# The seven-product stage of a fused attention and MoE kernel: g kept in PSUM, products in offset pairs

## Chip, cores and metric

One core of a Trainium2 chip. The metric is the device time of one execution in microseconds. Before the change the median of three runs is 555.94 us (554.25 to 556.14).

## The reference, cut to what matters

Windowed attention with sink tokens gives x, a soft mixture of experts turns x into its output, and a last layer follows. Only that last layer is changed. With n = 3072 tokens, model width 512 and inner width 2048:

```
c = row softmax of (x @ phi)              # 3072 x 32
x = c @ slot_out                          # 3072 x 512
h = x @ w_in                              # 3072 x 2048
g = h - tanh(h)
out = g @ w_out                           # 3072 x 512, float32
```

The kernel never forms x: it multiplies w_in with slot_out first and gets h from the 32 columns of c.

## The kernel before, in words

**Layout.** Output and g are held transposed: channels on the 128 partitions, tokens on the free axis. Inner channels come in 16 blocks f of 128. One h matmul (`cT`, `wst`, 96 rows: high and low parts of c and w stacked) gives one block of 128 inner channels by 512 tokens in one PSUM bank (`h_b`, two banks). ACT computes tanh in place and then u, a scaled square of it; DVE multiplies u and h to g (`g_mul`, L1280). g is split for TensorE into a rounded part gh (ACT, L1494 and L1601) and the rest gl = g - gh (L1451, which calls `arith`, L1444). gh and gl have five buffers each (`NG`). The weights w_out are loaded as 64-bit words, converted on DVE (L113 to L132, with a square on ACT), and split the same way into `whi` and `wlo`. One multiplication by g is three matmuls of 128 x 512: whi gh, wlo gh, whi gl.

**Regular steps.** The first 1024 tokens go in 32 steps (`steps`, L1194; N = 32): a step is one f, one chunk c of 512 tokens, four output blocks, 12 matmuls into `acc[0..3]`. A group of steps ends with an eviction of the four banks, added to a sum in SBUF (L1474 to L1491). Steps up to 5 are written out by hand (L1302); from step 6 on PE's work is ordered by the planner.

**Seven products.** The other 2048 tokens, in two halves (c = 1, 2) of 1024, use a scheme of seven products instead of eight (Winograd's form of Strassen's). A11, A12, A21, A22 are quarters of g (tokens halved, inner channels halved), S1 = A21 + A22, S2 = S1 - A11, S3 = A11 - A21, S4 = A12 - S2. On the weights' side T1 to T4 stand for B11 to B22 in the same way; T3 and T4 are prepared from w_out during the regular steps, T1 and T2 are split afresh at each use (`tsplit`, L1631). A product has 8 inner blocks i; a unit is one product and one i: 6 matmuls into two banks. There are 112 units. Before, they run as P4 and P5 alternating, then P7 and P1, then P6, P2 and P3 in turn, for each half; six banks accumulate (`acc`, `y_t`, `cv_t`), two hold h. At the end of each product its two banks are copied (ACT, L1668) or combined with earlier results (`comb`, L1623) and results are stored.

**Where g lies.** For the products g is written into one of 19 SBUF buffers (`place`, L1566). The low parts (L1450) and the sums S1 to S4 (L1595) then read two SBUF operands, and may go to POOL or DVE.

**What sets the order.** `_Order` (L142) is a list planner: each task has a due time, one or several engines with a cost from `US` (L59), and the buffers it reads and writes. `emit` simulates the engines and fixes each engine's program. The engines then run their programs in order, with semaphores. The due time of regular step i is 3.0 i, of product units 1.5 us apart (`op`, L1437). How far ahead of its use each stage stands is set by constants: `RL` and `WL` (L60, L61), and `TLAG` for the preparation of T3 and T4 (L1724). At an any-engine task the planner counts 0.69 us for DVE and 1.29 for POOL:

```
def arith(at, dst, a, b, rd, wr, alu=ALU.subtract, half=False, engs=("POOL", "DVE")):
    us = {"POOL": 0.67 if half else US["p"], "DVE": 0.4 if half else US["v"]}
    td.any_of(at, {e: (us[e], lambda e=e: names[e].tensor_tensor(dst, a, b, op=alu)) for e in engs}, rd, wr)
...
g = (g_b[k % 3], f"g{k % 3}")
...
add(t, "DVE", US["v"], [hn, un], [g[1]] + ([] if fast else ["z", "mk"]), lambda h=h, u=u, g=g: g_mul(h, u, g[0], fast))
```

A second copy of the program, for inputs that leave the small range of h or other window sizes, stands behind a branch that is not taken here (`fast` false).

Of the kernel before, what the change touches and what calls it, by code (L numbers as in the profile page):

```python
# [210 lines left out]
def tile_kernel(ctx: ExitStack, tc: tile.TileContext, qk, vv, v0, v0t, nw, phi, w1, w2,  # L211
# [17 lines left out]
    def run(ctx, fast):  # L229
# [1041 lines left out]
        def g_mul(h, u, g, small, fills=()):  # L1271
# [7 lines left out]
            if small:  # L1279
                DVE.tensor_tensor(g, u, h, op=ALU.mult)  # L1280
                fill()
            else:
                DVE.tensor_scalar(mk, u, TB * TB, None, op0=ALU.is_gt)
                DVE.tensor_scalar(z, u, TB * TB, None, op0=ALU.min)
                DVE.tensor_scalar(u, z, cg[6], None, op0=ALU.mult)
                for q in (5, 4, 3, 2, 1, 0):
                    DVE.scalar_tensor_tensor(u, u, cg[q], z, op0=ALU.add, op1=ALU.mult)
                fill()
                DVE.tensor_tensor(g, u, h, op=ALU.mult)
                ACT.activation(z, h, AF.Tanh)  # L1290
                DVE.tensor_tensor(z, h, z, op=ALU.subtract)
                DVE.copy_predicated(g, mk, z)
# [163 lines left out]
        for s in range(max(s0 - DL - 1, 0), N):  # L1456
            c, f, first, last = steps[s]
            t, x = op(s), s % NG
            gh, gl = gh_b[x], gl_b[x]
            wh, wl = whl[f]  # L1460
            W_ = [f"w{f}h", f"w{f}l"]
            for q in range(4):
                r = slice(P * q, P * q + P)

                def hi(q=q, r=r, wh=wh, wl=wl, gh=gh, first=first):
                    mm(acc[q], wh[:, r], gh, first, False)
                    mm(acc[q], wl[:, r], gh, False, False)
# [4 lines left out]
                add(t + 0.01 * q, "PE", 2 * US["mm"], [f"gh{x}"] + W_, [f"a{q}"], hi)
                add(t + (0.01 * q + 0.005 if last else 1.5 + 0.01 * q), "PE", US["mm"], [f"gl{x}"] + W_, [f"a{q}"], lo)
            if last:  # L1474
                fresh = (c, f) in ((0, 1), (1, 3))
                for q in range(4):
                    sp, o, b = sp_b[c % 2][q], acc[q], f"sp{c % 2}{q}"
                    at = t + 2.2 + 0.2 * q
                    if not fresh and (q % 2 == 0 or not fast):
                        add(at, "DVE", US["v"], [f"a{q}", b], [b], lambda sp=sp, o=o: DVE.tensor_tensor(sp, o, sp, op=ALU.add))  # L1480
                    elif q % 2 == fresh:
                        add(at, "DVE", US["v"], [f"a{q}"], [b], lambda sp=sp, o=o: DVE.tensor_copy(sp, o))
                    elif fresh:
                        add(at, "ACT", US["ev"], [f"a{q}"], [b], lambda sp=sp, o=o: ACT.copy(sp, o))
                    else:
                        m, n = (z, "z") if q == 1 else (mk.bitcast(F32), "mk")
                        add(at, "ACT", US["ev"], [f"a{q}"], [n], lambda m=m, o=o: ACT.copy(m, o))
                        add(at + 0.5, "POOL", US["p"], [n, b], [b], lambda sp=sp, m=m: POOL.tensor_tensor(sp, sp, m, op=ALU.add))
                    if f == 15:
                        add(at + 1.0, "SP", 0.1, [b], [f"out{c}{q}"],  # L1490
                            lambda sp=sp, q=q, c=c: SP.dma_start(out[P * q:P * q + P, CK * c:CK * c + CK], sp))  # L1491
            if s >= max(s0 - 1, 0):
                g = g_b[s % 3]
                add(t - RL["cast"], "ACT", US["cast"], [f"g{s % 3}"], [f"gh{x}"], lambda g=g, gh=gh: ACT.copy(gh, g))  # L1494
                split_lo(t - RL["lo"], g, f"g{s % 3}", x)

        prod = []
        for s in range(s0, N):
            prod.append((op(s), RL, s))
        need = {"A22": "P4", "A21": "P5", "A11": "P7", "A12": "P2"}  # L1500
        units = []
        for c in (1, 2):
            for a, n in ((0, 2), (2, 2), (4, 3)):
                units += [(c, MULT[a + j], i) for i in range(8) for j in range(n)]
        at_u = {(c, p[0], i): op(N + k) for k, (c, p, i) in enumerate(units)}
        gs = []
        for c in (1, 2):
            gs += [(c, a, i) for i in range(8) for a in ("A22", "A21")]
            gs += [(c, a, i) for a in ("A11", "A12") for i in range(8)]
        due = [at_u[c, need[a], i] - (1.5 if a in ("A21", "A11") else 0) for c, a, i in gs]  # L1510
        for j in range(len(gs) - 2, -1, -1):
            due[j] = min(due[j], due[j + 1] - GGAP)
        prod += [(t, WL, k) for t, k in zip(due, gs)]
        prod.sort(key=lambda e: e[0] - e[1]["h"])
        n = s0 + 1
        done = {}
        for t, L, k in prod:
            if L is RL and k == s0:
                done[k] = k
            elif not fast and L is RL and k == 1:  # L1520
                done[k] = k
            else:
                n = max(n, 1 if fast else 2)
                done[k] = n
                n += 1
        left = list(raw_f)
        blocks = {}

        def g_mul_at(k):
            if k in range(N):  # L1530
                return g_b[k % 3], f"g{k % 3}"
            return blocks[k]

        ev, muls = [], {}
        for t, L, k in prod:
            m = done[k]
            th = max(t - L["h"], muls.get(m - 2, -99.0) + 0.01)
            ta = max(t - L["act"], th + 0.3)
            tm = muls[m] = max(t - L["mul"], ta + 1.2, muls.get(m - 1, -99.0) + 0.01)
            assert tm < t - 4.7, (k, t, tm)  # L1540
            h, u, hn, un = h_b[m % 2], u_b[m % 3], f"h{m % 2}", f"u{m % 3}"
            if k in range(N):
                c, f = steps[k][:2]
                tok = CK * c
            else:
                c, a, i = k
                f = i + 8 * (a in ("A12", "A22"))
                tok = 1024 * c + CK * (a in ("A21", "A22"))
            x = f if f < 2 else 2 if f < 4 else 2 + f // 4
            if k not in range(s0 + (1 if fast else 2)):  # L1550
                add(th, "PE", US["h"], [f"wst{x}{q}" for q in range(3)], [hn],
                    lambda h=h, f=f, tok=tok: PE.matmul(h, w_of(f), cT[0:G3, tok:tok + CK], start=True, stop=True))  # L1552
            add(ta, "ACT", US["act"], [hn], [hn, un], lambda h=h, u=u: h_act(h, u, fast))
            ev.append((tm, "mul", k, (h, u, hn, un)))
        for k, (c, p, i) in enumerate(units):
            t = at_u[c, p[0], i]
            if p[1][0] == "S":
                ev.append((t - WL["sum"], "sum", (c, p[1], i), None))
            ev.append((t - WL["cast"], "cast", (c, p, i), N + k))
            ev.append((t - WL["lo"], "lo", (c, p, i), N + k))  # L1560
        ev.sort(key=lambda e: e[0])
        pool_, here = [(b, f"raw{b_}") for b_, b in enumerate(raw_f)], {}
        pool_ += [(b, n) for b, n in ((wf_b[8], "wfr0"), (wf_b[9], "wfr1"), (wf_b[10], "wfr2"), (cv_b[0], "cv0"))]
        pool_ += [(g_b[x], f"g{x}") for x in range(3)]

        def place(k):  # L1566
            here[k] = pool_.pop(0)

        for t, kind, k, arg in ev:
            if kind == "mul":  # L1570
                h, u, hn, un = arg
                if k in range(N):
                    g = (g_b[k % 3], f"g{k % 3}")
                else:
                    place(k)
                    g = here[k]
# [59 lines left out]
        for k, (c, p, i) in enumerate(units):  # L1636
# [11 lines left out]
            for ct in range(2):  # L1648
# [12 lines left out]
                if i < 7:  # L1661
                    continue
# [175 lines left out]
```

## Time and profile before

| | |
|---|---|
| median of three runs | 555.94 us |
| profiled execution, its own time | 555.75 us |
| span of its instructions | 554.0 us |
| busy, share of the span: PE, DVE, ACT, POOL | 90%, 84%, 71%, 65% |
| mean granted TensorE clock | 0.979 |

The span is the time from the first to the last instruction of the profiled execution. PE is TensorE's matmuls, PEld its weight loads, DVE VectorE, ACT ScalarE, POOL GpSimd, SPq the queue that issues the DMAs. Matmuls overlap in the pipeline: a matmul row lasts 0.39 us, but they start 0.23 us apart, so PE's busy share overstates its work and starts have to be counted. The clock is the granted share of full speed (1.00 is 2.4 GHz, 0.50 is 1.2 GHz).

### The profile page before, as it was taken

How to read it: one execution, taken by the hardware profiler on the slowest of the kernel's cores; microseconds unless marked ns; L12 is line 12 of the kernel's file. 1: busy time of each engine (PE TensorE's matmuls, PEld its weight loads, DVE VectorE, ACT ScalarE, POOL GpSimd, SP SyncE). 2: the span in 40 equal slices, each digit the busy share in tenths (PEclk: the TensorE clock that was granted, in tenths of full speed). 3: DMA queues.
4: the chain of work that ended last, by engine and by line, in shares of the span. 5: the costliest groups of instructions: out<-in, count | busy, mean ns of one | idle time of the engine just before them, and what ended most of it. 6: DMA issues, size and time to landing. Idle time of an engine off the chain costs nothing.

```text
span 554.0 us, 10289 instructions
## 1 busy us (share of the span) xinstructions
PE 496.3 (90%) x3554; PEld 337.3 (61%) x3554; DVE 466.6 (84%) x822; ACT 392.2 (71%) x1092; POOL 361.5 (65%) x383
## 2 busy tenths in 40 slices
PE   8798999999989998899898799998899989999991
PEld 4555556555545532466586567776578768776870
DVE  3999998998796496689997598889987998998676
ACT  4798998898895342388786569877688667857640
POOL 0466766656633000059999998698958798998972
PEclk9999999999999999899999889999999999999996
DMA  8979896434558999924310001200000021000004
GB/s 307 411 276 354 290 325 200 134 108 146 200 174 272 353 389 409 410 75 146 114 38 1 0 1 40 91 25 0 0 1 2 1 95 58 0 1 1 1 1 155
DMA packets 21995, 77.60 MB, mean 140 GB/s; under 512 B 2866, under 2 KB 4018, under 8 KB 20018
## 3 DMA queue, kind: packets, MB, share of 16 engines
q1 hardware_dynamic: 21938, 76.89, 38.2%
q8 instruction: 29, 0.48, 0.4%
q14 instruction: 28, 0.23, 0.1%
HBM read 70.59 MB, written 6.29 MB: 139 GB/s over the span
## 4 chain that ended last, share of the span: by engine, by line
PE 33%; DVE 25%; POOL 18%; DMA 9%; ACT 8%; issue 6%; SPq 0%; DVEq 0%; POOLq 0%; ACTq 0%
PE o L1454 12%; DMA w<-in_w 4%; DVE gl L1444 4%; POOL gl L1444 3%; PE av L728 3%; ACT w L664 3%; PE y L1454 3%; POOL wx L1444 3%; PE cvt L1454 3%; DVE mx L655 3%; PE h L1552 3%; PE o L1037 2%; DMA w<-in_qk 2%; DVE w L710 2%; DVE w L1444 2%
## 5 line engine op out<-in xcount | busy, mean ns | idle before, releaser
L1454 PE MATMUL o<-gh,whi 128*128 128x512 f32 x200 | 80.1, 400 | 3.4 <-DVE xt L1480 1.5
L1454 PE MATMUL o<-gh,wlo 128*128 128x512 f32 x200 | 79.2, 396 | 0.0
L674 POOL TENSOR_TENSOR w<-w,su 128x528 f32<-128x528 f32 x38 | 41.2, 1085 | 53.9 <-DVE su L671 36.6
L1454 PE MATMUL o<-gl,whi 128*128 128x512 f32 x200 | 67.1, 402 | 5.4 <-POOL gl L1444 5.3
L1255 ACT ACTIVATE h<-h 128x512 f32<-128x512 f32 x96 | 56.0, 583 | 16.1 <-PE h L1552 15.4
L1601 ACT CAST gh<-w 128x512 fp32r<-128x512 f32 x71 | 42.5, 617 | 26.2 <-DVE w L1444 12.0
L664 ACT ACTIVATE w<-w,nb 128x132 f32<-128x132 f32 x152 | 59.7, 393 | 1.2
L1256 ACT ACTIVATE u<-h 128x512 f32<-128x512 f32 x96 | 57.5, 599 | 3.0
L1444 POOL TENSOR_TENSOR gl<-w,gh 128x512 fp32r<-128x512 f32 x31 | 46.4, 1502 | 16.0 <-ACT gh L1601 13.6
L1444 DVE TENSOR_TENSOR gl<-w,gh 128x512 fp32r<-128x512 f32 x40 | 49.1, 1237 | 8.9 <-ACT gh L1601 8.7
L728 PE MATMUL av<-w,w 128*64 128x256 f32 (+1 forms) x448 | 48.3, 344 | 0.0
L1552 PE MATMUL h<-cT,wst 96*128 96x512 f32 x86 | 36.2, 421 | 13.5 <-DVE w L1280 7.4
L1454 PEld LDWEIGHTS o<-gl,whi 128*128 128x128 f32 x200 | 38.1, 191 | 16.6 <-POOL gl L1444 8.2
L634 PE MATMUL sc<-w 64*64 64x200 f32 (+2 forms) x768 | 45.5, 331 | 2.6 <-DMA w<-in_qk 1.7
L1454 PEld LDWEIGHTS o<-gh,whi 128*128 128x128 f32 x200 | 38.1, 191 | 14.1 <-DVE xt L1480 2.1
L1105 POOL TENSOR_SCALAR whi<-wx 128x512 fp32r<-128x512 f32 x6 | 3.9, 645 | 61.6 <-DVE so L1165 60.0
L1454 PEld LDWEIGHTS o<-gh,wlo 128*128 128x128 f32 x200 | 38.2, 191 | 8.2
L634 PEld LDWEIGHTS sc<-w 64*64 64x64 f32 x768 | 26.5, 132 | 15.8 <-issue 10.1
L728 PEld LDWEIGHTS av<-w,w 128*64 128x64 f32 x448 | 25.8, 136 | 15.3 <-issue 9.2
L1444 POOL TENSOR_TENSOR gl<-g,gh 128x512 fp32r<-128x512 f32 x23 | 32.4, 1415 | 3.2 <-ACT gh L1601 3.1
L1280 DVE TENSOR_TENSOR w<-u,h 128x512 f32<-128x512 f32 x44 | 29.8, 677 | 4.6 <-ACT u L1256 4.2
L710 DVE TENSOR_TENSOR w<-pT,c_t 128x512 f32<-128x512 f32 x46 | 31.2, 679 | 0.0
(435 smaller groups left out, 1385.9 us busy)
## 6 DMA issues: line engine op xcount, KB each, us to landing
w<-in_w SPq DMA_DIRECT2D x32, 512.0 KB, 10.2
w<-in_w SPq DMA_DIRECT2D x14, 1024.0 KB, 7.0
w<-in_qk SPq DMA_DIRECT2D x16, 780.0 KB, 6.7
w<-in_w_out SPq DMA_DIRECT2D x15, 512.0 KB, 3.6
w<-in_vv SPq DMA_DIRECT2D x16, 384.0 KB, 4.3
w<-in_w_in SPq DMA_DIRECT2D x8, 512.0 KB, 5.3
out<-xt SPq DMA_DIRECT2D x12, 256.0 KB, 2.2
win_t<-in_w_in SPq DMA_DIRECT2D x4, 512.0 KB, 9.8
```

The source lines that it names most:

```text
L634: PE.matmul(sc_t[i][u][w, o:o + n], a[r, 64 * j:64 * j + 64], kslc(a, lo, n)[r, :], start=True, stop=True)
L664: ACT.activation(Z[:, u, :], Z[:, u, :], AF.Exp, bias=nb[:, u:u + 1], scale=SCALE, accum_out=su[:, u, :])
L674: (POOL if i < NQ - 1 else DVE).tensor_tensor(Z, Z, su.to_broadcast([P, 4, CH]), op=ALU.mult)
L710: DVE.tensor_tensor(d[:, :, 0, :], src, mL, op=ALU.mult)
L728: PE.matmul(dst[r, :], v[:, t, r], l, start=start, stop=stop, skip_group_check=True)
L1255: ACT.activation(h, h, AF.Tanh, scale=ca)
L1256: ACT.activation(u, h, AF.Square, scale=cc ** 0.5)
L1280: DVE.tensor_tensor(g, u, h, op=ALU.mult)
L1444: td.any_of(at, {e: (us[e], lambda e=e: names[e].tensor_tensor(dst, a, b, op=alu)) for e in engs}, rd, wr)
L1454: PE.matmul(o, w, a, start=start, stop=stop)
L1552: lambda h=h, f=f, tok=tok: PE.matmul(h, w_of(f), cT[0:G3, tok:tok + CK], start=True, stop=True))
L1601: add(t, "ACT", US["cast"], [gn], [f"gh{x}"], lambda g=g, x=x: ACT.copy(gh_b[x], g))
```

## The change

g of A22, A11 and A12 is multiplied in place into the PSUM bank of its h and stays there until its split and its sums are done; A21, S1 and the sums that follow lie in SBUF. From regular step 11 (`RPS`) the steps' g stays in its bank too. h has four banks: y joins at the start, cvt when the weights are converted. A low part with a PSUM operand goes to DVE, one from SBUF to POOL; S1 to S4 go to DVE. The products run in seven pairs (`PAIRS`), the second one unit behind the first, on two pairs of accumulators (`acc[0..3]`). The rounding of T1 and T2 is pinned to POOL; copies of P4, P5 and P1 may go to ACT or DVE. tanh and square are two tasks. The converted weights 13 to 15 go to three further buffers, and T3 and T4 are prepared later (`TLAG`, `TLAG2`). The planner's costs are new. The fixed list of due times (`prod`, `gs`, `ev`) gives way to a queue of events, in which a stage is put down when its buffer is there (`produce`, `act`, `mul`, `ssum`, `cast`, `unit`). The diff, cut:

```diff
-EPS_T = 0.15
-US = {"mm": 0.2275, "h": 0.24, "act": 1.19, "cast": 0.615, "v": 0.69, "p": 1.29, "pc": 0.62, "ev": 0.5, "sq": 0.69}
...
-TLAG = 6.0
+EPS_T = 0.0
+US = {"tanh": 0.6, "mm": 0.229, "h": 0.24, "act": 1.2, "cast": 0.62, "v": 0.695, "vs": 1.2, "vs2": 0.75, "p": 1.31, "p2": 0.72, "pc": 0.64, "ev": 0.6, "sq": 0.69}
+LEAD, RCAST, SCAST, TCAST = 10.0, 6.0, 4.0, 4.0
+RPS = 11
+GGAP = 2.2
+TLAG = 12.0
+TLAG2 = 4.0
+PAIRS = (((1, "P4"), (1, "P5")), ((1, "P7"), (1, "P1")), ((1, "P6"), (1, "P2")), ((1, "P3"), (2, "P4")),
+         ((2, "P5"), (2, "P1")), ((2, "P7"), (2, "P6")), ((2, "P2"), (2, "P3")))
...
         def arith(at, dst, a, b, rd, wr, alu=ALU.subtract, half=False, engs=("POOL", "DVE")):
-            us = {"POOL": 0.67 if half else US["p"], "DVE": 0.4 if half else US["v"]}
+            us = {"POOL": US["p2"] if half else US["p"], "DVE": US["v"] if len(engs) == 1 else US["vs2"] if half else US["vs"]}
...
-        def split_lo(at, g, gn, x):
-            arith(at, gl_b[x], g, gh_b[x].bitcast(F32), [gn, f"gh{x}"], [f"gl{x}"])
...
+        FRESH = {"A21": (), "A22": ("P4", "S1"), "A11": ("P1", "S3", "S2"), "A12": ("P2", "S4")}
...
+        idle_h = [(y_t, "y"), hs[n0 % 2]] if fast else [(y_t, "y")]
...
+        def produce(at, j):
...
+                if not idle_h or (k[0] != "r" and k[1] == "A21" and not spare):
+                    return later(at, lambda at: produce(at, j))
+                b = bank[k] = idle_h.pop(0)
...
+        def act(at, k, b, u, un):
+            if fast:
+                add(at, "ACT", US["tanh"], [b[1]], [b[1]], lambda: ACT.activation(b[0], b[0], AF.Tanh, scale=ca))
+                add(at + 0.1, "ACT", US["cast"], [b[1]], [un], lambda: ACT.activation(u, b[0], AF.Square, scale=cc ** 0.5))
...
+        def mul(at, k, b, u, un):
+            if k[0] == "r" and k[1] < RPS:
...
+                here[k] = (g_b[x % 3], f"g{x % 3}")
+            elif k[0] == "r" or k[1] != "A21":
+                here[k] = b
+            d = here[k]
+            add(at, "DVE", US["v"], [b[1], un], [d[1]] + ([] if fast else ["z", "mk", un]), lambda: g_mul(b[0], u, d[0], fast))
...
+            if d is not b:
+                release(k)
...
+        def ssum(at, k, then):
...
+            wait = {"S2": (c, "P5", i), "S4": (c, "P6", i)}.get(o)
...
+            arith(at, d[0], x[0], y[0], [x[1], y[1]], [d[1]], alu, engs=("DVE",))
...
+        def cast(at, u, k, then):
+            if u - NG > ran[0]:
+                return later(at, lambda at: cast(at, u, k, then))
...
+            add(at, "ACT", US["cast"], [gn], [f"gh{x}"], lambda: ACT.copy(gh_b[x], g))
+            psum = gn[0] in "hyc" and gn != "cv0"
...
+                arith(at, gl_b[x], g, gh_b[x].bitcast(F32), [gn, f"gh{x}"], [f"gl{x}"], engs=("DVE",) if psum else ("POOL",))
...
-        ba, by, bb = ((acc[0], "a0"), (acc[1], "a1")), ((y_t, "y"), (cv_t, "cvt")), ((acc[2], "a2"), (acc[3], "a3"))
...
+        two = [[(acc[x], f"a{x}"), (acc[x + 1], f"a{x + 1}")] for x in (0, 2)]
...
-                    add(at, "ACT", US["ev"], [b[1]], [d[1]], lambda d=d, b=b: ACT.copy(d[0], b[0]))
+                    td.any_of(at, {"ACT": (US["ev"], lambda d=d, b=b: ACT.copy(d[0], b[0])),
+                                   "DVE": (US["v"], lambda d=d, b=b: DVE.tensor_copy(d[0], b[0]))}, [b[1]], [d[1]])
...
-                    wf[f] = wf_b[f if f < 8 else 8 + f % 3]
+                    wf[f] = wf_b[f] if f < 8 else wf_b[8 + f % 3] if f < 13 else raw_f[f - 7]
...
-                        tb += TLAG
+                        tb += TLAG if f < 13 else TLAG + TLAG2 * (f - 12)
...
+        push(op(26), lambda at: idle_h.append((cv_t, "cvt")))
```

## Rows read from the trace of the kernel before

**Rows 1.** Stretches: busy us of PE, PEld, DVE, ACT, POOL; granted clock; DMA share, GB/s.
```profile
260.30:356.00 95.70, 85.87 (x346) 65.46 (x345) 81.50 (x117) 70.58 (x128) 86.16 (x94) 0.96 0.12 39
356.00:541.00 185.00, 171.95 (x724) 135.01 (x723) 164.51 (x179) 129.56 (x238) 156.81 (x123) 0.99 0.05 18
...
300.00:330.00 30.00, 24.57 (x90) 18.03 (x89) 20.57 (x30) 16.91 (x32) 28.53 (x32) 0.89 0.00 0
```
**Rows 2.** The h matmuls of the planner's part, line 1552: durations, first and last start.
```profile
L1552 PE MATMUL h<-cT,wst x86: 392/393/628, 262.5 to 529.4; 96*128 96x512 f32 x86
```
**Rows 3.** Timeline of PE: start us, us, engine, line, operation.
```profile
278.70 0.40 PE L1454 MATMUL o<-gh,whi 128*128 128x512 f32 x1
...
287.68 0.40 PE L1454 MATMUL o<-gh,whi 128*128 128x512 f32 x1
...
316.17 0.80 PE L1454 MATMUL o<-gl,whi 128*128 128x512 f32 x1 [2.80 <-POOL gl L1444]
...
322.37 0.39 PE L1454 MATMUL o<-gl,whi 128*128 128x512 f32 x1
```
**Rows 4.** PE's waits, 260.3 to 356 us: total us, times, longest.
```profile
PE o L1454 <- POOL gl L1444: 5.2, 3, 2.8
PE h L1552 <- DVE g L1280: 1.8, 3, 1.0
```
**Rows 5.** PE's waits, 356 to 545 us.
```profile
PE h L1552 <- DVE w L1280: 6.8, 5, 2.6
PE h L1552 <- DVE g L1280: 3.9, 3, 2.2
PE o L1454 <- ACT v_t L1668: 1.3, 1, 1.3
```
**Rows 6.** Groups, 356 to 541 us: count, busy us, mean ns, idle before.
```profile
L1444 DVE TENSOR_TENSOR gl<-w,gh 128x512 fp32r<-128x512 f32 x39 | 47.7, 1233 | 8.9 <-ACT gh L1601 8.7
L1444 POOL TENSOR_TENSOR gl<-w,gh 128x512 fp32r<-128x512 f32 x30 | 45.1, 1509 | 14.8 <-ACT gh L1601 12.4 <-PE y L1454 2.4
L1601 ACT CAST gh<-w 128x512 fp32r<-128x512 f32 x68 | 40.8, 618 | 26.2 <-DVE w L1444 12.0 <-POOL w L1444 6.9 <-PE o L1454 6.1
...
L1256 ACT ACTIVATE u<-h 128x512 f32<-128x512 f32 x54 | 32.3, 599 | 1.7
L1255 ACT ACTIVATE h<-h 128x512 f32<-128x512 f32 x54 | 31.5, 583 | 12.7 <-PE h L1552 12.3
...
L1280 DVE TENSOR_TENSOR w<-u,h 128x512 f32<-128x512 f32 x34 | 23.0, 676 | 2.2 <-ACT u L1256 2.0
...
L1668 ACT COPY xt<-o 128x512 f32<-128x512 f32 x4 | 2.4, 595 | 0.0
```
**Rows 7.** Groups, 260.3 to 356 us.
```profile
L1444 DVE TENSOR_TENSOR gl<-g,gh 128x512 fp32r<-128x512 f32 x10 | 10.1, 1007 | 0.1
L118 DVE SCALAR_TENSOR_TENSOR cvt<-w,cvt 128x512 uint32<-128x512 uint32 x10 | 6.9, 692 | 0.2
```
**Rows 8.** Timeline, 385 to 389 us: DVE and, below it, POOL.
```profile
385.54 0.68 DVE L1444 TENSOR_TENSOR wf<-wf,w 128x512 f32<-128x512 f32 x1
...
387.46 1.78 DVE L1444 TENSOR_TENSOR gl<-g,gh 128x512 fp32r<-128x512 f32 x1
...
386.90 1.80 POOL L1444 TENSOR_TENSOR cv<-cv,w 128x512 f32<-128x512 f32 x1 [2.16 <-DVE w L1280]
```
**Rows 9.** POOL's groups, 260.3 to 300 us.
```profile
L1444 POOL TENSOR_TENSOR gl<-g,gh 128x512 fp32r<-128x512 f32 x5 | 6.4, 1289 | 0.1
...
L1444 POOL TENSOR_TENSOR wlo<-wx,whi 128x256 fp32r<-128x256 f32 x3 | 2.2, 744 | 0.2
...
L1448 POOL TENSOR_SCALAR t4hi<-wf 128x256 fp32r<-128x256 f32 x3 | 1.5, 512 | 0.3
```
**Rows 10.** Timeline of the end: the last matmul and DVE's last operations.
```profile
541.65 0.39 PE L1454 MATMUL o<-gl,whi 128*128 128x512 f32 x1
...
547.91 1.27 DVE L1444 TENSOR_TENSOR xt<-o,xt 128x512 f32<-128x512 f32 x2
```

More of the change, by code (lines that the diff above doesn't have):

```diff
@@ L1450, in split_lo, with rounded @@
-        def split_lo(at, g, gn, x):
-            arith(at, gl_b[x], g, gh_b[x].bitcast(F32), [gn, f"gh{x}"], [f"gl{x}"])
+        def rounded(at, dst, src, rd, wr, half=False, engs=("ACT", "POOL")):
+            ways = {"ACT": (0.36 if half else US["cast"], lambda: ACT.copy(dst, src)),
+                           "POOL": (0.36 if half else US["pc"], lambda: POOL.tensor_scalar(dst, src, 1.0, 0.0, op0=ALU.mult, op1=ALU.add))}
+            td.any_of(at, {e: ways[e] for e in engs}, rd, wr)
         def mm(o, w, a, start, stop):
@@ L1454, in mm @@
             PE.matmul(o, w, a, start=start, stop=stop)
-        for s in range(max(s0 - DL - 1, 0), N):
+        SUM = {"S1": ("A21", "A22", ALU.add), "S3": ("A11", "A21", ALU.subtract),
+               "S2": ("S1", "A11", ALU.subtract), "S4": ("A12", "S2", ALU.subtract)}
+        FRESH = {"A21": (), "A22": ("P4", "S1"), "A11": ("P1", "S3", "S2"), "A12": ("P2", "S4")}
+        prods = {p[0]: p for p in MULT}
+        units = [("r", s) for s in range(N)]
+        for (c, p), (d, q) in PAIRS:
+            xs = [(c, p, i) for i in range(8)]
+            ys = [(d, q, i) for i in range(8)]
+            seq = xs[:1]
+            for i in range(1, 8):
+                seq += [xs[i], ys[i - 1]]
+            units += seq + ys[7:]
@@ new lines, in run @@
+        number = {u: k for k, u in enumerate(units)}
+        due = {("r", s): op(s) for s in range(s0, N)}
+        for c in (1, 2):
+            for i in range(8):
+                due[c, "A22", i] = op(number[c, "P4", i])
+                due[c, "A21", i] = due[c, "A22", i] - 0.5
+                due[c, "A11", i] = min(op(number[c, "P1", i]), op(number[c, "P7", i]) - 1.5)
+                due[c, "A12", i] = op(number[c, "P2", i])
+        gs = sorted(due, key=lambda k: due[k])
+        for j in range(len(gs) - 2, -1, -1):
+            due[gs[j]] = min(due[gs[j]], due[gs[j + 1]] - (0.5 if gs[j + 1][0] == "r" else GGAP))
@@ new lines, in run, with later, release, g_spec @@
+        bank, here, useq = {("r", s0): hs[s0 % 2]}, {}, [s0]
+        if not fast:
+            bank["r", 1] = hs[1]
+        ran = [max(s0 - DL - 1, 0) - 1]
+        def later(at, fn):
+            push(at + 0.2, fn)
+        def release(k):
+            idle_h.append(bank[k])
+        def g_spec(k):
+            if k[0] == "r":
+                c, f = steps[k[1]][:2]
+                return f, CK * c
+            c, a, i = k
+            return i + 8 * (a in ("A12", "A22")), 1024 * c + CK * (a in ("A21", "A22"))
@@ new lines, in ssum @@
+        def ssum(at, k, then):
+            c, o, i = k
+            a, b, alu = SUM[o]
+            ka, kb = (c, a, i), (c, b, i)
+            wait = {"S2": (c, "P5", i), "S4": (c, "P6", i)}.get(o)
+            if ka not in seen or kb not in seen or (wait and ("split", number[wait]) not in seen) or (o == "S1" and not spare):
+                return later(at, lambda at: ssum(at, k, then))
+            if o == "S1":
+                here[k] = spare.pop(0)
+            else:
+                here[k] = here[{"S3": (c, "A21", i), "S2": (c, "S1", i), "S4": (c, "S2", i)}[o]]
+            x, y, d = here[ka], here[kb], here[k]
+            arith(at, d[0], x[0], y[0], [x[1], y[1]], [d[1]], alu, engs=("DVE",))
+            seen.add(k)
+            then()
+            u = number[{"S1": (c, "P5", i), "S3": (c, "P7", i), "S2": (c, "P6", i), "S4": (c, "P3", i)}[o]]
+            push(max(at + 0.7, op(u) - SCAST), lambda at: cast(at, u, k, lambda: None))
@@ L1457, in run, with unit, regular @@
+        def unit(at):
+            k = ran[0] + 1
+            if k == len(units):
+                return
+            u = units[k]
+            if k >= max(s0 - 1, 0) and ("split", k) not in seen:
+                return later(at, unit)
+            ran[0] = k
+            if u[0] == "r":
+                regular(at, u[1])
+            else:
+                product(at, u, k)
+            push(max(at + (3.0 if u[0] == "r" else 1.37), op(k + 1)), unit)
+        def regular(t, s):
             c, f, first, last = steps[s]
-            t, x = op(s), s % NG
+            x = s % NG
@@ L1470, in lo @@
                     mm(acc[q], wh[:, r], gl, False, last)
[L1472 to L1563, printed above, removed]
@@ new lines, in regular @@
+            for q in range(4):
+                sp, o, b = sp_b[c % 2][q], acc[q], f"sp{c % 2}{q}"
+                at = t + 0.7 + 0.6 * q
+                if not fresh and (q % 2 == 0 or not fast):
+                    add(at, "DVE", US["v"], [f"a{q}", b], [b], lambda sp=sp, o=o: DVE.tensor_tensor(sp, o, sp, op=ALU.add))
+                elif q % 2 == fresh:
+                    add(at, "DVE", US["v"], [f"a{q}"], [b], lambda sp=sp, o=o: DVE.tensor_copy(sp, o))
+                elif fresh:
+                    add(at, "ACT", US["ev"], [f"a{q}"], [b], lambda sp=sp, o=o: ACT.copy(sp, o))
+                else:
+                    m, n = (z, "z") if q == 1 else (mk.bitcast(F32), "mk")
+                    add(at, "ACT", US["ev"], [f"a{q}"], [n], lambda m=m, o=o: ACT.copy(m, o))
+                    add(at + 0.5, "POOL", US["p"], [n, b], [b], lambda sp=sp, m=m: POOL.tensor_tensor(sp, sp, m, op=ALU.add))
+                if f == 15:
+                    add(at + 1.0, "SP", 0.1, [b], [f"out{c}{q}"],
+                        lambda sp=sp, q=q: SP.dma_start(out[P * q:P * q + P, CK * c:CK * c + CK], sp))
@@ L1610, in run @@
+        two = [[(acc[x], f"a{x}"), (acc[x + 1], f"a{x + 1}")] for x in (0, 2)]
+        where = {}
+        for xy in PAIRS:
+            for x, p in enumerate(xy):
+                where[p] = two[x]
         wt = {}
@@ L1686, in run, with t_fresh @@
                     store(at + 1.0, t5, 2 + ct, c, 0)
-        qn = {}
+        nt = 0
+        for k, u in enumerate(units):
+            if u[0] != "r" and prods[u[1]][2] in ("T1", "T2"):
+                j, o, i = nt % 3, 0 if u[1] == "P5" else 256, u[2]
+                nt += 1
+                push(op(k) - TCAST, lambda at, j=j, o=o, i=i, m=nt: t_fresh(at, j, o, i, m))
+        def t_fresh(at, j, o, i, m):
+            if m - 3 > ntr[0]:
+                return later(at, lambda at: t_fresh(at, j, o, i, m))
+            tsplit(at, wf_b[i][:, o:o + 256], f"wf{i}" + ("r" if o else "l"), tr[j][0], f"tr{j}h", tr[j][1], f"tr{j}l", ("POOL",))
         for s, todo in plan.items():
```

172 lines of the change are left out of this document (101 added, 71 removed).

## The prediction

> **What bounds the kernel now.** I read the stretches first, then the matmul cadence, then the waits of TensorE (PE), then the groups of instructions, last the tail. The stretch of the planner's matmuls starts at 260.3 us [rows 1]; all before it is code that the diff does not touch, so 260.3 us is a fixed term. From there the planner orders 26 regular steps of 12 matmuls, 112 product units of 6, and the h matmuls, 86 of them [rows 2]: 312 + 672 + 86 = 1070. With nothing in the way a step of 12 and its h repeats every 2.99 us: three steps, 39 matmuls, run from 278.70 to 287.68 [rows 3], 0.2303 us a slot. So 1070 slots are 246.4 us, and PE could be done at 506.7 us; it is done at 542.0 [rows 10]. Of the 35.3 us lost, 16.0 lie in the regular stretch (95.7 us for 346 matmuls, 79.7 us of slots), 18.3 in the product stretch (185 us for 724, 166.7 us of slots) [rows 1], 1.0 in the last microsecond of matmuls. PE is busy most of the time, but it is not alone: DVE is busy 164.5 and POOL 156.8 of the 185 us.
>
> What PE waits for says which. Regular stretch: 5.2 us for a low part (gl) from POOL, 1.8 for DVE to free an h bank [rows 4]. After the longest wait PE came back slow: in the slice 300 to 330 the granted clock is 0.89 [rows 1], and 14 matmuls from 316.17 to 322.37 took 6.2 us instead of 3.2 [rows 3]: 3.0 more. Product stretch: 10.7 us at an h matmul for DVE's multiplication, which frees one of only two h banks, and 1.3 for an eviction [rows 5].
>
> Why are DVE and POOL late? A DVE operation with both operands in SBUF takes 0.68 us where POOL stands still beside it (at 385.54), 1.78 where POOL runs one (at 387.46) [rows 8]. The low part, gl = g - gh, is such an operation; its mean on DVE is 1.23, and POOL's is 1.51 in the product stretch against 1.29 where DVE mostly has one operand in PSUM [rows 6, 9]. DVE with one PSUM operand takes 0.68 in every group: the multiplication, the conversions that read and write PSUM [rows 6, 7]. So the two engines hold each other up over SBUF, and two-thirds of a microsecond is the bare price. The Trainium skill (SBUF — State Buffer, section on the two separate sides) says the same as a rule: a DVE operation with two SBUF inputs and a GpSimd operation exclude each other for the whole instruction. The trace agrees with it: 0.68 beside 1.78.
>
> **The change part by part.**
> *Splits and sums from PSUM.* g of A22, A11 and A12 is multiplied into its own h bank and stays there. Per 1024 tokens, 24 low parts (P4, P1, P2) and all 32 sums then have one PSUM operand, on DVE at 0.68; the 32 low parts of S1 to S4 are on POOL alone, and from step 11 the regular steps' low parts are on DVE from PSUM. The sums of the product stretch by engine: DVE, 54 multiplications, 48 low parts and 64 sums, 166 x 0.68 = 113 us, and 20 combinations that read a result bank, 14: 127 us where 164.5 stand now. POOL, 64 low parts at 1.29 = 83, 32 splits of T1 and T2 (hi 0.51, lo 0.74 [rows 9]) at 1.25 = 40 together, and up to 12 SBUF combinations, 15: 138 us against 156.8. ACT keeps its work, 54 x 1.18 for tanh and square, 112 casts at 0.62, 12 copies at 0.60 [rows 6]: 140 us. A cast out of PSUM has no row; the copy out of PSUM (0.60) is the nearest above nothing, the SBUF cast (0.62) the other end; I take 0.62. A multiplication that reads and writes PSUM has as nearest row the conversion cvt<-w,cvt, 0.69 [rows 7]. PE needs 166.7. So each of the three comes under PE; now DVE and POOL together do not.
>
> A rule speaks against moving operands to PSUM. The rows show none of it: 0.677 with one PSUM operand, 0.69 with two SBUF operands and POOL idle [rows 6, 8]. The Trainium skill (Perfetto Trace Analysis, Optimizing Scalar/DVE Operations) gives DVE some 125 ns of access overhead on PSUM against 60 on SBUF; by it the 112 operations would cost an estimated 7 us more of DVE, which would still leave DVE under PE.
>
> *Four h banks.* y, later cvt, join the two. The 1.8 and the 10.7 us of waiting for a bank go if four banks suffice. The chain on one bank is h 0.39, tanh 0.58, square 0.60, multiplication 0.68, cast 0.62, low part 0.68: 3.6 us, 4.2 with a sum. Where A22 and A21 are both made (two of the seven pairs) two units, 14 slots or 3.2 us, bring one bank of 4.2 and one of 2.3: 6.5 us on four banks is 1.6 of 3.2. The new wait is this: an h matmul stands in PE's queue until a bank is released by a sum or a split, and the products behind it wait too. It is the rival below.
>
> *Regular stretch.* POOL loses the low parts from step 11 on, some 11 x 1.29 [rows 9] = 14 of its 86.2 us, and with them the 5.2 us wait and the slow 3.0 us; DVE exchanges 10 low parts, 10.1 us [rows 7], for about 21 at 0.68, 14.3. DVE then stands at 86 us and POOL at 72, and the planner may move the weights' low parts from the one to the other. Evictions stay. For them and small gaps I leave 4 us of the present 16: what is over when 5.2, 1.8 and 3.0 are gone is 6.0, and fewer stops leave fewer gaps behind them. That makes 83.7 us. Bounds: 79.7, and 90 if DVE and POOL, 158 us together, are filled only to the 88% of today (167.7 of 191).
>
> *Preparation of T3 and T4 later* (TLAG 12, more for the last three weights): four half subtractions at 0.74 and two half splits at 1.25 [rows 9], 5.5 us of POOL for each weight, moved behind work that PE waits for. First used in pair 1 and 2, one i every two units; nothing, and if POOL is full, it shows as a wait for t4 or whi.
>
> *Products in offset pairs on four accumulators.* Same 672 matmuls. When the first of a pair is done, 12 matmuls, 2.8 us, of its partner run before the bank is wanted; two copies need 1.2, the four combinations of P7 2.7. I leave the present 1.3 us of eviction waits. POOL is the tight one in the pair P7, P6 of the second half, which has two POOL low parts each i: 16 x 1.29 + 8 x 0.51 = 24.7 us, 30.6 if the T2 low parts stay on POOL too, against 96 slots, 22.1. I take 3 us. With 2 us of small gaps, 6.3 us are lost of the present 18.3: bounds 0 and 18.3.
>
> *The tail.* Now P6, P2 and P3 end together: from the last matmul's end, 542.0, DVE's list of combinations runs on until 549.2, and the last store lands 4.8 us later [rows 10]. After the change only P2 and P3 are last, P2 two units earlier; behind the last matmul stand one combination, 0.68, and a store, 4.8 as now: 5.5 instead of 12.0 us. SP's queue holds only stores there, four fewer.
>
> **Sum.** 506.7 + 4 + 6.3 = 517.0 for the last matmul, + 5.5 = 522.5 us span. The profiled execution took 555.75 for its span of 554.0, so 524.3, and that execution lies 0.2 us under the median of 555.94: 524.
>
> **Rivals.**
> *POOL stays slow* (0.18). If POOL's low parts remain at 1.80 as beside DVE now [rows 8], the pair P7, P6 takes 16 x 1.80 + 8 x 1.25 = 38.8 us, 13.7 beyond the 25.1 that I allowed, and P6 with P2 some 4 more: 542. For it: POOL at 1.5 on average now. Against: 1.29 where DVE reads PSUM [rows 9].
> *Only the order at the end counts* (0.06). If the waits were latency of the chain h, tanh, square, multiplication, cast, and not the two engines' hold on each other, only the tail's 6.5 us come: 549. For it: DVE's and POOL's low parts stand 8.9 and 14.8 us idle for ACT's cast in the product stretch [rows 6]; against: the bare chain is 3.6 us.
> *Banks held too long* (0.07), slower. In the product stretch 64 values pass four banks. The kernel is slower than before by over 0.5% when that stretch exceeds 207.5 us (558.7 less 1.75, 5.5, 260.3 and 83.7), a mean hold of 4 x 207.5 / 64 = 13.0 us. At 13.5 the time is 567. For it: PE already waits for banks, and a hold now includes a sum that waits for another product's split. Against: the chain is 4.2, and two banks with 54 values in 185 us held each under 6.9. The Trainium skill (PSUM — Partial Sum Buffer, summary of rules) advises to evacuate promptly, which this change does not; no row here shows a hold through splits.
>
> **Chances.** The forecast 0.62, the rivals 0.18, 0.06 and 0.07, mixtures near no change 0.07 (0.05 within 0.5%, 0.02 faster). About 0.5%, 2.8 us, is what a measurement here can tell from nothing. Faster 0.88, same 0.05, slower 0.07. The range runs from no loss beside the slots (506.7 + 5.5 + 1.75 = 514, less 1 for the spread of the runs) to the first rival: 513 to 542.
>
> **What would show it.** DVE's low parts and sums at 0.68 and POOL's at 1.3; PE waiting for h under 3 us in all; no slice of the product stretch with a clock under 1.00; regular stretch near 84, product stretch near 173 us, last matmul near 517, 5.5 us behind it. Wrong if PE waits for h again (banks), if POOL's gl ends PE's waits (first rival), or if the regular stretch stays at 95.

## The result and the profile after

The changed kernel takes 524.68 us in the median of four runs (524.13 to 525.41); the ratio to the kernel before is 0.945, 95% interval 0.9425 to 0.947. The prediction was 524 us. The span of the profiled execution is 522.4 us, 31.6 less than before, with a granted clock of 0.994.

The two stretches of the planner's part, cut where the first matmul of each starts and the last one ends (us, then busy time of PE, PEld, DVE, ACT and POOL with counts, granted clock, DMA share, GB/s), answer to [rows 1]:

```profile
260.50:345.00 84.50, 80.56 (x346) 64.24 (x345) 74.17 (x117) 65.17 (x119) 76.48 (x99) 1.00 0.14 44
345.00:517.10 172.10, 170.30 (x728) 134.72 (x726) 129.52 (x197) 126.31 (x230) 124.16 (x127) 1.00 0.08 28
```

The matmuls are as many as before, the clock is full in both, and DVE and POOL have fallen well under PE: in the product stretch 129.5 and 124.2 us where they had 164.5 and 156.8, beside 728 slots of 0.2303 us, 167.7 us.

PE's waits in the two stretches, which answer to [rows 4, 5]:

```profile
PE o L1456 <- ACT whi L1451: 2.0, 1, 2.0
PE y L1525 <- DVE gl L1448: 1.6, 1, 1.6
PE o L1456 <- POOL gl L1448: 0.3, 1, 0.3
...
PE o L1456 <- POOL gl L1448: 0.7, 3, 0.3
PE o L1456 <- DVE gl L1448: 0.7, 1, 0.7
PE o L1456 <- ACT gh L1594: 0.4, 1, 0.4
```

The 10.7 us of waiting at h in the product stretch are gone, and so is the 5.2 us wait for POOL in the regular one. What is left in the regular stretch is one wait for a rounded weight (`whi`) and one at h (its matmul into bank y), for a low part that still held the bank.

Groups of the profile's page, for the whole execution, which answer to [rows 6] (count, busy us, mean ns, idle before):

```profile
L1448 POOL TENSOR_TENSOR gl<-w,gh 128x512 fp32r<-128x512 f32 x39 | 50.7, 1311 | 15.8 <-ACT gh L1594 12.4
...
L1284 DVE TENSOR_TENSOR h<-u,h 128x512 f32<-128x512 f32 x39 | 26.8, 689 | 16.4 <-ACT u L1537 16.3
...
L1594 ACT CAST gh<-h 128x512 fp32r<-128x512 f32 x39 | 22.9, 587 | 12.5 <-DVE h L1284 4.8
...
L1448 DVE TENSOR_TENSOR gl<-h,gh 128x512 fp32r<-128x512 f32 x39 | 26.6, 684 | 3.8 <-ACT gh L1594 3.4
```

DVE's low part from a PSUM bank costs 0.684 us where the SBUF one cost 1.233 [rows 6], and POOL's is down from 1.509 to 1.311. The few two-operand SBUF instructions that DVE keeps in the product stretch still pay:

```profile
L1448 DVE TENSOR_TENSOR trlo<-wx,trhi 128x256 fp32r<-128x256 f32 x3 | 3.7, 1244 | 1.7 <-POOL trhi L1452 1.7
...
L1448 DVE TENSOR_TENSOR xt<-q,xt 128x512 f32<-128x512 f32 x2 | 3.6, 1797 | 0.0
```

The low part of a half split, 256 columns, costs 1.24 us there, nearly twice a full one from PSUM.

The end on the timeline, which answers to [rows 10] (start us, us, engine, line, operation):

```profile
516.42 1.37 DVE L1448 TENSOR_TENSOR xt<-o,xt 128x512 f32<-128x512 f32 x2 [1.35 <-PE o L1456]
516.67 0.39 PE L1456 MATMUL o<-gl,whi 128*128 128x512 f32 x1
517.14 1.01 SPq L1684 DMA_DIRECT2D out<-xt  x2
```

The last matmul ends at 517.06 us; 0.73 us later DVE is done, 4.6 us after that the span ends: 5.3 us of tail instead of 12.0. The order of the products does this, not the place of the operands: in the run below with the products' g back in SBUF the last matmul ends at 540.2 us and the span at 545.6, again 5.3 us later; with the old order and the new prices alone the tail is still 9.8.

So the 31.6 us come from three places: the regular stretch 95.7 to 84.5, 11.2; the product stretch 186.0 (356.0 to 542.0) to 172.1, 13.9; the tail 6.7; the start of the first stretch lies 0.2 later.

### The profile page after: what moved, and what is told of

Read it like the earlier page. It is cut to its first block, busy times and chain, and to the rows that moved or that the text cites. A ratio compares the mean times of both kernels' runs of the same rounds, so it can differ in the third digit from the quotient of the medians.

```text
span 522.4 us, 10288 instructions
## 1 busy us (share of the span) xinstructions
PE 489.3 (94%) x3554; PEld 335.0 (64%) x3554; DVE 416.8 (80%) x832; ACT 383.9 (73%) x1075; POOL 315.8 (60%) x390
## 4 chain that ended last, share of the span: by engine, by line
PE 47%; POOL 19%; DVE 14%; DMA 8%; ACT 7%; issue 3%; SPq 0%; POOLq 0%; DVEq 0%; ACTq 0%
PE o L1456 28%; PE av L732 3%; POOL wlo L1448 3%; POOL gl L1448 3%; ACT w L668 3%; POOL wx L1448 3%; DVE mx L659 3%; PE o L1041 3%; DMA w<-in_w_out 2%; DMA w<-in_w 2%; DMA w<-in_qk 2%; DVE w L714 2%; PE sc L638 2%; DMA w<-in_vv 2%; POOL gl L1270 2%
## 5 line engine op out<-in xcount | busy, mean ns | idle before, releaser
L1456 PE MATMUL o<-gh,whi 128*128 128x512 f32 x232 | 91.8, 396 | 2.4 <-ACT whi L1451 2.0
L1456 PE MATMUL o<-gh,wlo 128*128 128x512 f32 x232 | 91.0, 392 | 0.0
L1456 PE MATMUL o<-gl,whi 128*128 128x512 f32 x232 | 74.8, 393 | 1.2 <-DVE gl L1448 0.7
L1448 POOL TENSOR_TENSOR gl<-w,gh 128x512 fp32r<-128x512 f32 x39 | 50.7, 1311 | 15.8 <-ACT gh L1594 12.4
L1284 DVE TENSOR_TENSOR h<-u,h 128x512 f32<-128x512 f32 x39 | 26.8, 689 | 16.4 <-ACT u L1537 16.3
L638 PEld LDWEIGHTS sc<-w 64*64 64x64 f32 x768 | 26.5, 132 | 15.7 <-issue 10.3
L732 PEld LDWEIGHTS av<-w,w 128*64 128x64 f32 x448 | 25.8, 136 | 15.3 <-issue 9.2
L1536 ACT ACTIVATE h<-h 128x512 f32<-128x512 f32 x45 | 26.4, 587 | 9.8 <-PE h L1525 9.5
L1594 ACT CAST gh<-h 128x512 fp32r<-128x512 f32 x39 | 22.9, 587 | 12.5 <-DVE h L1284 4.8
L1448 DVE TENSOR_TENSOR gl<-h,gh 128x512 fp32r<-128x512 f32 x39 | 26.6, 684 | 3.8 <-ACT gh L1594 3.4
L700 PE MATMUL pT<-c_t,w 128*128 128x128 f32 x148 | 23.6, 282 | 6.3 <-POOL w L678 3.9
L652 ACT COPY w<-sc 128x264 f32<-128x264 f32 x63 | 21.2, 372 | 10.7 <-PE sc L768 6.2
L1594 ACT CAST gh<-w 128x512 fp32r<-128x512 f32 x39 | 24.1, 621 | 6.0 <-PE o L1456 4.8
## 6 DMA issues: line engine op xcount, KB each, us to landing
w<-in_w SPq DMA_DIRECT2D x32, 512.0 KB, 10.2
```

The source lines that it names most:

```text
L638: PE.matmul(sc_t[i][u][w, o:o + n], a[r, 64 * j:64 * j + 64], kslc(a, lo, n)[r, :], start=True, stop=True)
L652: ACT.copy(z, base)
L700: PE.transpose(pt[:, P * u:P * u + P], Z[:, u, 0:P], ident)
L732: PE.matmul(dst[r, :], v[:, t, r], l, start=start, stop=stop, skip_group_check=True)
L1456: PE.matmul(o, w, a, start=start, stop=stop)
L1536: add(at, "ACT", US["tanh"], [b[1]], [b[1]], lambda: ACT.activation(b[0], b[0], AF.Tanh, scale=ca))
```

## The experiments

Theory A is the prediction's: the gain in the stretches comes from the place of the operands, since DVE and POOL no longer hold each other up. Theory B: the planner's new prices do it, whatever lies where. Theory C: the additional h banks do it. The pairs belong to theory C's side of the change: they accumulate in four banks instead of six, and that is what leaves y and cvt free for h.

**Prices alone (theory B), in the kernel before.**

```diff
-EPS_T = 0.15
+EPS_T = 0.0
...
-            us = {"POOL": 0.67 if half else US["p"], "DVE": 0.4 if half else US["v"]}
+            us = {"POOL": 0.72 if half else US["p"], "DVE": US["v"] if len(engs) == 1 else 0.75 if half else 1.2}
```

> The kernel before with the new planner costs alone: a two-operand DVE task counts 1.2 us (0.75 for a half) instead of 0.69 (0.40), a half on POOL 0.72, and ties go to the earliest start. All data stay where they were. Theory A (operands: DVE and POOL hold each other up over SBUF, and the change frees them by giving g a PSUM operand): the work is the same, so the time stays within 1.5% of before, 547 to 563 us, with DVE's low parts still near 1.2 and POOL's near 1.5. Theory B (the planner had wrong prices, and right ones make the order that the chip can follow): most of the gain without the data moved, 528 to 540 us.

Measured: 558.15 us, ratio 1.0023 (1.0007 to 1.0039). DVE and POOL together are as full as before; the two stretches, 96.7 and 190.6 us:

```profile
259.50:356.20 96.70, 86.31 (x347) 64.56 (x346) 81.34 (x113) 71.17 (x131) 89.67 (x93) 0.98 0.12 40
356.20:546.80 190.60, 176.75 (x727) 137.33 (x725) 154.26 (x165) 130.47 (x242) 181.49 (x139) 0.97 0.04 16
```

The truer price moves work from DVE (154.3 us) to POOL (181.5) and gains nothing. Theory B falls: the prices alone do not do it.

**The products' g back in SBUF, all else as changed (theories A and C).**

```diff
-            elif k[0] == "r" or k[1] != "A21":
+            elif k[0] == "r":
                 here[k] = b
+            elif k[1] != "A21":
+                if len(spare) < 2:
+                    return later(at, lambda at: mul(at, k, b, u, un))
+                here[k] = spare.pop(0)
...
-                        release(k)
+                        spare.append(here[k])
...
-            arith(at, d[0], x[0], y[0], [x[1], y[1]], [d[1]], alu, engs=("DVE",))
+            arith(at, d[0], x[0], y[0], [x[1], y[1]], [d[1]], alu)
```

(A low part of the products may go to POOL or DVE.)

> The changed kernel with one thing undone: g of A22, A11 and A12 is multiplied into an SBUF buffer and its h bank is freed at once; the low parts and the sums of the products then have two SBUF operands and may go to POOL or DVE. Four h banks, offset pairs, planner costs and the regular steps stay as in the changed kernel. Theory A: the product stretch goes back from 172 to 180 to 188 us, DVE's low parts and sums cost 1.1 to 1.3 and POOL's 1.5, the regular stretch stays at 85; in all 532 to 541 us. Theory B, and theory C (four h banks are what counts, as they let TensorE run ahead): 523 to 528 us.

Measured: 547.39 us, ratio 0.9845 (0.9824 to 0.9866). The regular stretch is the changed kernel's, the product stretch takes 194.6 us; stretches, then PE's longest waits in the second, then two groups of it:

```profile
260.50:345.60 85.10, 81.18 (x348) 64.58 (x347) 74.79 (x114) 65.81 (x120) 81.02 (x101) 1.00 0.13 43
345.60:540.20 194.60, 179.53 (x726) 138.52 (x724) 166.69 (x172) 129.17 (x231) 186.92 (x151) 0.96 0.07 25
...
PE o L1456 <- POOL gl L1448: 10.6, 10, 2.7
...
L1448 POOL TENSOR_TENSOR gl<-w,gh 128x512 fp32r<-128x512 f32 x42 | 63.0, 1507 | 0.8 <-ACT gh L1598 0.8
...
L1448 DVE TENSOR_TENSOR gl<-w,gh 128x512 fp32r<-128x512 f32 x26 | 32.9, 1271 | 5.7 <-PE o L1456 3.3 <-ACT gh L1598 2.4
```

Four banks, pairs and new planner are there, yet POOL is busy for 186.9 of 194.6 us, PE waits for it, and the low parts cost 1.27 us on DVE and 1.51 on POOL, about as before the change (1.23 and 1.51 [rows 6]). Theory C alone falls too: more banks without the operands give nothing in this stretch. A's direction holds, but its price was set too low (541 at most). That may lie in the new price, which fills POOL; so the same again with the old one:

```diff
-            us = {"POOL": US["p2"] if half else US["p"], "DVE": US["v"] if len(engs) == 1 else US["vs2"] if half else US["vs"]}
+            us = {"POOL": US["p2"] if half else US["p"], "DVE": US["v"] if len(engs) == 1 else 0.4 if half else 0.69}
```

> The run with the products' g in SBUF (547 us) again, with the planner's old prices for DVE's two-operand work (0.69, 0.40 a half) instead of 1.2 and 0.75, so that low parts and sums are shared out between DVE and POOL as before the change. In that run POOL was busy 187.5 of 195 us, and DVE 167. Theory A (the operands cost, and the rest over the expected 541 us was the sharing that the new price made): product stretch 180 to 190 us, 533 to 542 us. Rival (any sharing ends at the same sum, since what one engine is spared the other has to wait for): 544 to 550 us.

Measured: 544.43 us, ratio 0.9806 (0.9769 to 0.9843).

```profile
260.30:349.50 89.20, 82.58 (x347) 65.53 (x345) 74.70 (x116) 67.24 (x122) 79.24 (x99) 0.98 0.13 42
349.50:536.90 187.40, 174.32 (x725) 137.06 (x725) 175.71 (x197) 125.85 (x226) 156.48 (x128) 0.98 0.07 26
```

The product stretch came out as A said, 187.4 us, now with DVE the fuller one; but the old price also cost the regular stretch 4.1 us, 89.2 for 85.1, which no theory had in it, and the total lies in the rival's range. With either sharing the product stretch is longer than with g in PSUM, by 15.3 and 22.5 us, and no shorter than before the change (186.0). So the rest of the change gives nothing there without the operands: the whole 13.9 us hang on them. They are not the operands' alone, as the runs on banks and on the offset below show.

The kernel before shows the hold itself. From 260 to 545 us, among DVE's two-operand instructions of 128 x 512 that stand singly in its timeline, the 11 with both operands in SBUF that ran while POOL stood still took 0.68 to 0.69 us; 93 of the same kind beside a POOL instruction took 1.16 in the mean, up to 1.79; 99 with an operand in PSUM beside a POOL instruction took 0.67 to 0.69. POOL's own of this size took 1.30 us in the mean with no DVE instruction on two SBUF operands beside them (19), 1.58 with one (83). The time for which an instruction is held up thus counts as its busy time.

**The regular steps' g in SBUF.** Here `RPS = 11` becomes `RPS = 32`; the products keep g in PSUM. Three runs: the first also moves three SBUF buffers ahead in the list of spare ones, the second does not, the third holds h back while three values of u are under way.

> The changed kernel with the g of all regular steps in SBUF, as before the change (RPS 32 instead of 11), so that their 21 low parts go back to POOL at 1.3 us, 27 us more POOL work; the products keep g in PSUM. Theory A: POOL is over-full in the regular stretch (76.6 + 27 us in a stretch of 85), which grows to 92 to 100 us with waits of TensorE for POOL's gl, the product stretch stays at 172: 531 to 540 us. Theory B: 523 to 527 us.

> The run with all regular steps' g in SBUF again, with the SBUF buffers handed out in the order of the changed kernel (in the earlier run of this kind the buffers of the last converted weights were handed out too early, which changed values in T3 and T4, not the work). The regular stretch took 92 us in that run, the time was 532.9: 530 to 536 us again.

> The run with all regular steps' g in SBUF (RPS 32) once more, with h held back until one of the three buffers of u is free: in the two earlier runs of this kind some multiplications could take the u of a later step, which changes values, not the work. Theory A: as there, POOL and DVE fill the regular stretch, 91 to 96 us instead of 84.5, the product stretch stays at 172: 531 to 537 us. Rival (those runs were slow because h came too early, not because of where g lies): 524 to 528 us.

Measured: 532.86, 532.88 and 532.78 us, ratios 0.9582 (0.9563 to 0.9601), 0.9597 (0.9563 to 0.9631) and 0.9593 (0.9559 to 0.9628). In these runs the last regular step multiplies by the u of another value: the planner's list hands u's three buffers out in turn, and that step's multiplication comes after the next use of its buffer. In the third run ACT starts to write this u at 330.31 us, and the multiplication starts at 345.26, with four more values of u written between. So the buffers named in the second text were not the reason, and the third run's guard, a count, does not prevent it. The work is of the same kind and size. The third run's stretches:

```profile
260.30:353.40 93.10, 85.63 (x349) 65.09 (x347) 82.53 (x116) 71.82 (x135) 86.92 (x91) 0.98 0.12 40
353.40:526.00 172.60, 169.70 (x725) 134.70 (x725) 125.41 (x192) 124.04 (x226) 125.26 (x129) 1.00 0.07 27
```

The regular stretch is 93.1 us with DVE and POOL at 82.5 and 86.9, nearly the 81.5 and 86.2 of before [rows 1]; the product stretch stays at 172.6. So 8.6 of the 11.2 us of the regular stretch hang on the place of g. That is the hold and the moved work together: with g in SBUF these low parts go to POOL alone (24 at 1.39 us), and this run does not tell the two apart.

**Banks.** Two banks (y and cvt do not join), then three (cvt does not):

```diff
-        idle_h = [(y_t, "y"), hs[n0 % 2]] if fast else [(y_t, "y")]
+        idle_h = [hs[n0 % 2]] if fast else [(y_t, "y")]
...
-        push(op(26), lambda at: idle_h.append((cv_t, "cvt")))
+        push(op(26), lambda at: None if fast else idle_h.append((cv_t, "cvt")))
```

> The changed kernel with two h banks instead of four (y and cvt do not join). Theory A with the bank holds of the prediction: 64 values hold a bank for 2.3 us (A21) or some 4.2 to 5.5 us (the others) on two banks, which is 64 values x 4.5 / 2 = 144 us of the 172 at best and more than the room in the two pairs that make A22 and A21; a wait of TensorE at h returns in both stretches: 540 to 565 us. Theory B: 524 to 528 us.

> The changed kernel with three h banks (cvt does not join; until step 26 the changed kernel has three as well). Theory A, with two banks at 543 us and four at 525: if values hold a bank for about 4.5 to 5.5 us in the mean, 64 of them on three banks are 96 to 117 us of a stretch of 172, so room remains outside the two pairs that make A22 and A21, and 3 to 8 us are lost there: 526 to 533 us. If one bank more were enough for all: 524 to 526 us.

Measured: 542.88 us with two, ratio 0.9757 (0.9741 to 0.9773); 524.37 with three, ratio 0.9449 (0.9424 to 0.9474), the same as with four. With two banks the product stretch takes 187.9 us, with DVE and POOL busy only 132.1 and 126.9; the first line is PE's longest wait in it, the next two ACT's:

```profile
348.40:536.30 187.90, 175.75 (x734) 134.67 (x732) 132.08 (x204) 134.25 (x240) 126.87 (x131) 1.00 0.07 25
...
PE o L1456 <- ACT gh L1594: 10.1, 12, 1.6
...
ACT h L1536 <- PE h L1525: 15.4, 24, 1.6
ACT gh L1594 <- PE o L1456: 8.2, 13, 0.8
```

Neither of them is full: g comes too late through the chain, ACT waits for h and PE for ACT's gh. The time is in the range of the text, but the wait of PE at h that it named did not return (0.2 us); by its code the planner puts h down only once it expects a bank free. A kept g needs the third bank, worth 18 us in all and 15.8 in the product stretch, more than the 13.9 us that this stretch gained: the operands without the bank give nothing either. The fourth is worth nothing, and the text for three banks, which gave it 3 to 8 us, was wrong.

**Offset of the pairs** (`units += [xs[i], ys[i]]` for each i, instead of y one unit behind).

> The changed kernel with the two products of a pair alternating without the offset of one unit (the last unit of the first is followed by one unit, 6 matmuls or 1.4 us, not two). Theory A: two copies of 0.6 still fit, the four combinations of P7 (2.7 us) stand out by 1.3 us each time, and the tail grows by little: 526 to 530 us. Rival: the offset matters for nothing since TensorE has h matmuls and low parts to fill with: 524 to 526 us.

Measured: 529.50 us, ratio 0.9532 (0.9506 to 0.9559): 4.8 us more, as theory A had it. PE's waits in the product stretch:

```profile
PE o L1456 <- ACT gh L1592: 2.1, 1, 2.1
PE o L1456 <- POOL gl L1448: 1.4, 2, 1.1
PE o L1456 <- DVE mk L1448: 1.2, 2, 1.0
```

Only 1.2 us of them are for a combination (`mk` is one of P6); the order of the whole list changes with the offset, so that the 4.8 us are the edit's, but not shown to be P7's four combinations.

**T3 and T4 early** (`TLAG = 6.0`, `TLAG2 = 0.0`).

> The changed kernel with the preparation of T3 and T4 as early as before the change (lag 6 for all weights instead of 12 and more). Theory A as predicted (the lag costs and brings nothing): 523.5 to 526 us. Rival: the lag is what takes POOL's half subtractions out of the way of work that TensorE waits for, as POOL is 93% busy in the regular stretch; then the regular stretch grows by 2 to 6 us with waits for POOL's gl or for whi: 527 to 531 us.

Measured: 526.10 us, ratio 0.9469 (0.9443 to 0.9494), just above theory A's range and under the rival's; its interval overlaps that of the changed kernel. By the medians the later preparation is worth 1.4 us, which these runs do not tell from nothing.

**Where the regular steps change over** (`RPS = 9`, then 13).

> The changed kernel with the regular steps' g in PSUM from step 9 on instead of 11: two low parts move from POOL (1.3 us each) to DVE (0.68). Theory A: the one long wait left in the regular stretch, 2.0 us for whi at 274.8 us, stands in a slice in which DVE is 98% and POOL 98% busy; 2.6 us less POOL work there and 1.4 more of DVE change it by 1 us at most either way: 523 to 526 us.

> The changed kernel with the regular steps' g in PSUM from step 13 on (9 gave 527.3 us with a wait of 3.7 us of TensorE for an h bank that a low part held, 11 gives 524.7). Two low parts more on POOL at 1.3, two banks free earlier. If the early steps are limited by banks: 522 to 525 us; if by POOL, which is 96% busy to 300 us: 525 to 529 us.

Measured: 527.33 us, ratio 0.9493 (0.9469 to 0.9517), and 527.73, ratio 0.9501 (0.9466 to 0.9536). The first missed its text: the wait for whi is gone, and a longer one has come (PE's timeline):

```profile
322.25 0.39 PE L1456 MATMUL o<-gl,whi 128*128 128x512 f32 x1
326.31 0.80 PE L1525 MATMUL h<-cT,wst 96*128 96x512 f32 x1 [3.68 <-DVE gl L1448]
326.91 1.49 PE L1456 MATMUL o<-gl,whi 128*128 128x512 f32 x3
328.19 0.63 PE L1456 MATMUL o<-gh,whi 128*128 128x512 f32 x1
```

An h stands at the head of PE's queue until a low part frees its bank, and the products behind it stand too. With 13 PE waits 2.2 us for ACT's copies at an eviction and again 2.0 for whi; the time is in the range that the text gave to a limit by POOL, but these waits name ACT, so that cause is not shown. No run beats the changed kernel; three banks equal it.

## Why the prediction was right

**The slots.** 1070 matmuls of 0.2303 us from 260.3 us: the first starts at 260.5, and the last ends 10.2 us behind the 506.9 us that the slots alone would give from there. I had left 10.3.

**Regular stretch.** 83.7 us were forecast, 84.5 measured: 4.8 us lost instead of 4. The wait for POOL's low part went, 5.2 us to 0.3, and so did the slow clock behind it; the 1.8 us for a bank did not: a wait at h of 1.6 us stands there, now for a low part that holds the bank. What else is left were not the evictions that I had left in: no eviction shows among PE's waits, but whi (2.0) does. DVE was busy for 74.2 us where I had 86, POOL 76.5 for 72.

**Product stretch.** 173.0 us by the forecast's terms, 172.1 measured. The forecast loads were sums of durations. Neighbouring instructions of an engine overlap a little (DVE's rows of 0.68 us can start 0.60 apart), so the busy times of the first view are not the like of them; the rows added up are. So counted, DVE's load was 139.4 us for 127 forecast, too low, as DVE kept nine instructions with SBUF operands alone, 12 us, that I had given to POOL; POOL's was 127.0 for 138, ACT's 138.0 for 140. Of the prices, DVE's 0.68 became 0.684 and 0.689, POOL's 1.29 became 1.31; the cast out of PSUM, taken at 0.62 between 0.60 and 0.62, cost 0.587, under both ends. The 3 us for the pair P7 and P6, in which POOL has two low parts for each i, were not lost. POOL is full there and DVE empty, but PE is not held up:

```profile
470.00:490.00 20.00, 19.77 (x86) 15.65 (x85) 4.75 (x9) 11.52 (x20) 19.67 (x22) 1.00 0.00 1
```

86 matmuls in 20 us are 19.8 us of slots. That those 3 us and the eviction's 1.3 did not come, while other small stops did, let the sum of 6.3 us look better founded than it was (4.4 measured: 172.1 less 167.7).

**The tail.** 5.3 us for 5.5: one combination and a store.

**The mechanism.** The two engines' hold on each other is seen in the durations of the kernel before, and what it costs was shown by undoing the change: with the operands in SBUF the product stretch is 187 to 195 us, the regular one 93. By the Trainium skill (SBUF — State Buffer, section on the two separate sides) a DVE instruction with two SBUF inputs and a GpSimd instruction that reads SBUF exclude each other for the whole instruction. These runs agree with it: 1.16 us in the mean and up to 1.79 beside POOL, 0.68 to 0.69 with POOL idle or with an operand in PSUM. The Trainium skill (Perfetto Trace Analysis, Optimizing Scalar/DVE Operations) also has a PSUM access cost DVE some 65 ns more than one on SBUF. That shows in no duration here: 0.684 from PSUM against 0.68 to 0.69 undisturbed from SBUF.

**The part on banks** was half right. The product stretch needs more than two, as the chain of 3.6 to 4.2 us with its queues says; that all four count was wrong. The rival of banks held too long did not come, but its mechanism is real in two places: 1.6 us in the changed kernel, 3.7 when the steps change over at 9.

## What to carry to other kernels

When VectorE and GpSimd are both nearly full and their two-operand instructions last longer than the bare price, look where the operands lie before sharing the work out anew: prices alone gave nothing here, and some 22 of the 31.6 us (13.9 and 8.6) hang on one operand left in PSUM. Neither that operand without the third bank nor the banks without it shortened the product stretch. Count the banks that this takes by the chain until the last reader, and try one fewer. Then order the end, so that the outputs which need the fewest steps after their last matmul come last: 4.5 to 6.7 us here (9.8 or 12.0 us of tail in the old order, 5.3 in the new).

## What was not expected of the hardware

TensorE's clock answers to short stops in a way that a wait's length alone does not tell. In the changed kernel it stays at 1.00 through the wait of 2.0 us. With T3 and T4 early, two waits of 1.2 and 0.4 us stand one matmul apart, and the slice behind them (columns as in the stretches) is slow:

```profile
315.00:320.00 5.00, 5.00 (x17) 3.95 (x17) 5.00 (x10) 2.76 (x6) 4.92 (x5) 0.72 0.00 0
```

17 matmuls in 5 us are 0.29 us each; the matmuls from 314.74 to 317.30 us start 0.43 us apart, the lower of the two levels, and from 317.73 on 0.23 again. With the change-over at step 9 the 13 matmuls behind the 3.7 us wait, from 326.31 to 331.96 us, take 5.65 us instead of 3.0. So a stop that looks like 2 or 4 us is dearer where the clock falls, and that belongs in the price of a wait. Each of these is one profiled execution; the four of the changed kernel have mean granted clocks of 0.992 to 0.997, so the same program does not always lose the same, and no run here tells what decides it.
